# Block 2's tokens loaded as bands and turned by DMA transposes, as in the later blocks

## The chip, the cores and the metric

The kernel runs on one core of a Trainium2 chip. The metric is the device time of that core in microseconds. A core has TensorE (PE) for matmuls, VectorE (DVE), ScalarE (ACT), GpSimd (POOL) and SyncE (SP), and 16 DMA engines that move data between HBM and the on-chip memory. GpSimd, SyncE and ScalarE issue the transfers. Each engine works through its own instructions in order and waits on semaphores for the others.

## What is computed

Chunked attention, and a gated feed-forward layer on its output. There are 4 batches, 8 heads, 768 tokens and head size 64:

```python
for c in range(nc):                       # chunks of 32 queries
    l_start = max(0, 32 * c - 16)
    r_end = min(S, 32 * c + 32 + 8)
    k_full = concatenate([mem_k, k[:, :, l_start:r_end]])     # 8 memory rows + up to 56 keys
    v_full = concatenate([mem_v, v[:, :, l_start:r_end]])
    a = softmax(q_c @ k_full.T / sqrt(D))
    out[:, :, chunk] = a @ v_full
x = out as (3072 tokens, 512)
result = (maximum(x @ w_gate, 0) * (x @ w_val)) @ w_out       # w_gate, w_val 512x1536, w_out 1536x512
```

Inputs and output are float32. The kernel computes with float16 operands and float32 sums.

## The kernel before

The 3072 tokens are cut into 8 blocks of 384 (`TB`), two to a batch. A block's queries are four pieces of 96 (`NQ`, `QB`), and each piece looks at one window of 8 memory rows and 120 tokens, which fills the 128 partitions. Heads are handled as four pairs (`hp`).

*Feed-forward.* A block takes twelve units (`ffn_unit`), one for each 128 columns of the hidden layer: four gate matmuls and four value matmuls (L380), a Relu on ScalarE (L388, `gr`), and a product on VectorE (L392, `gv`). Three out units (`out_unit`, L416) then multiply `gv` with `wo`, copy the result on ScalarE and store it. The weights `wg`, `wv` and `wo` stay on chip. `wo` is loaded in three pieces of 512 KB.

*Attention.* For a head pair the steps are: scores and exponentials (`step_s`), values and sums with the logarithm of the sums (`step_v`: L344, L348), the reciprocal (`step_e`, L353), and the product into `xT` (`step_m`, L359). `xT` is what the block's units read. The attention of block n+1 is spread over the units of block n by `run(order, n, at, turn_at)`: `at[hp]` names the unit after which a pair's scores are computed. Values come two units later and the product three units later.

*How K and Q get their transposed form* differs between blocks.

- Blocks 0, 1 and 2 load rows of four tokens (`load_rows`: `rk`, `rq`). TensorE turns them with matmuls against selection matrices (`turn_k`, `turn_q`, L207), and VectorE copies the result (`copy_k`, `copy_q`, tile `kq`). Their scores are eight matmuls for a pair (`score_mms`, L263), each over the 64 rows of one head.
- Blocks 3 to 7 load windows of tokens (`load_band` and `load_q_tokens`: tiles `k16`, shown as `k`, and `q16n`; L145, L171). SyncE turns them by DMA transposes (`turn_dma`: `kT`, `qT`; L241, L243). GpSimd copies `qT` into a block-diagonal tile `qbd` (`spread_q`, L250), whose other halves were cleared once (`clear_q`, L659). The scores are then four matmuls for a pair over all 128 rows (L287).

*What sets the order.* The order is written by hand: under `manual_schedule` every engine runs its instructions in program order. Blocks 0 and 1 follow a list of named steps (`go`), and after them come the calls of `run`. All float32-to-float16 loads are issued by GpSimd, so its program order is also the order of these loads. A load waits for the landing of the load eight before it. `spread_q` stands in this same order. Block 2 is the only later block that is turned by matmuls inside `run`: its turns sit between the gate and value matmuls of block 1's units 1, 4, 7 and 10 (`turning`), and its scores follow units 2, 5, 8 and 11. GpSimd's order around the change is: block 2's rows, block 2's V (`vwin`), the three pieces of `wo`, block 3's K, q and V, and block 3's `spread_q`.

Of the kernel before, what the change touches and what calls it, by code (L numbers as in the profile page):

```python
# [8 lines left out]
F32 = mybir.dt.float32  # L9
# [8 lines left out]
def kernel(  # L18
# [99 lines left out]
    def rows_of(n):  # L118
        if n not in rows:
            rows[n] = (half.tile([KR + 2, H, J * D], F16, tag="rk", name="rk"),  # L120
                       half.tile([QR, H, J * D], F16, tag="q16", name="rq"))
        return rows[n]

    def load_rows_mem(dma, dst, n, h0, nh, src_t=mem_k):
        src = bass.AP(tensor=src_t.tensor, offset=src_t[n // 2, h0, 0, 0].offset,
                      ap=[[J * D, 2], [NMEM * D, nh], [1, J * D]])
        dma(dst, src)
# [7 lines left out]
    def load_rows(n, h0, nh):  # L135
        load_k(n, h0, nh)
        load_q(n, h0, nh)

    def load_band(n, src_t, dsts):
        b, p = divmod(n, 2)  # L140
        for i in range(NQ):
            m0, m1 = (16 if (p == 0 and i == 0) else 0), (112 if (p == 1 and i == NQ - 1) else BAND)
            src = bass.AP(tensor=src_t.tensor, offset=src_t[b, 0, TB * p + QB * i - 16 + m0, 0].offset,
                          ap=[[D, m1 - m0], [S * D, H], [1, D]])
            pool_dma(dsts[p][NMEM + m0:NMEM + m1, i, :, 0:D], src)  # L145
# [12 lines left out]
    def load_mem_v(n):  # L158
        b, p = divmod(n, 2)
        for i in range(NQ):  # L160
            sp(vwins[p][0:NMEM, i, :, 0:D], memv[:, H * b:H * b + H, :])
# [11 lines left out]
    def load_w(c0, c1):  # L173
        for dst, src in ((wg, moe_w_gate), (wv, moe_w_val)):
            pool_dma(dst[:, :, c0:c1], src.rearrange("(c p) f -> p c f", p=128)[:, :, c0:c1])
# [8 lines left out]
        return pools["f"].tile([128, 512], F32, tag="f", name=name)  # L184

    def turn_k(n, hp):
        if n != 1:
            pool, tag = (pools["t"], "t") if n == 0 else (pools["s"], "sc")
            ps = pool.tile([128, 2, 512], F32, tag=tag, name="kq_ps")
            kps, qps = ps[:, 0], xs if (n, hp) == (0, 0) else ps[:, 1, 0:TB]  # L190
        else:
            ps, kps, qps = None, bank("k_ps"), bank("q_ps")[:, 0:TB]
        turns[n, hp] = ps, kps, qps


        steps = kps.rearrange("p (i j t) -> p j i t", i=NQ, j=J) if n < 2 else kps.rearrange("p (j r) -> p j r", j=J)
        turn_mms(rows_of(n)[0], steps, sels[n % 2].rearrange("p i t -> p (i t)")[0:KR + 2], hp)

    def turn_q(n, hp):
        steps = turns[n, hp][2].rearrange("p (r j) -> p j r" if n == 0 else "p (j r) -> p j r", j=J)  # L200
# [2 lines left out]
    def turn_mms(t, steps, w, hp):  # L203
        t = t.rearrange("p h (j d) -> p h j d", j=J)
        for j in range(J):
            for hh in range(2):
                nc.tensor.matmul(steps[D * hh:D * hh + D, j], lhsT=t[:, 2 * hp + hh, j], rhs=w,  # L207
                                 start=True, stop=True)

    def kq_of(n):  # L210
        if n not in kTs:
            kq = turned.tile([128, HP, 512 + TB], F16, tag="kq", name="kq")
            kTs[n] = kq[:, :, 0:512].rearrange("p a (i m) -> p i a m", i=NQ)
            qTs[n] = kq[:, :, 512:].rearrange("p a (i m) -> p i a m", i=NQ)
            turns[n] = kq
        return turns[n]

    def copy_k(n, hp):
        src, dst = turns[n, hp][1], kq_of(n)[:, hp, 0:512]
        if n == 2:  # L220
            src, dst = src.rearrange("p (j r) -> p r j", j=J), dst.rearrange("p (r j) -> p r j", j=J)
        dve_copy(dst, src)  # L222

    def copy_q(n, hp):
        src, dst = turns[n, hp][2], kq_of(n)[:, hp, 512:]
# [4 lines left out]

    def copy_kq(hp):
        dve_copy(kq_of(0)[:, hp], turns[0, hp][0].rearrange("p a c -> p (a c)")[:, 0:512 + TB])

    def turn(n, hp):
        for step in (turn_k, turn_q, copy_k, copy_q):
            step(n, hp)

    def turn_dma(n):
        kTs[n] = turned.tile([128, NQ, HP, 128], F16, tag="kT", name="kT")
# [39 lines left out]

    def score(n, hp):  # L280
        sc = scs[n, hp] = pools["s"].tile([128, 2, 512], F32, tag="sc", name="sc_ps")
        if n < 3:
            score_mms(n, hp, sc, True)
        else:

            for i in range(NQ):
                nc.tensor.matmul(sc[:, i // 2, 192 * (i % 2):192 * (i % 2) + 192], lhsT=kTs[n][:, i, hp, :],  # L287
                                 rhs=qbds[n % 2][:, i, hp].rearrange("p h m -> p (h m)"), start=True, stop=True)

    def score_exp(n, hp):  # L290
        view = scs[n, hp][:, :, 0:TB].rearrange("p a (c m) -> p a c m", m=QB)
        if n < 3:
            flat = exs[n, hp] = epool.tile([128, 2, NQ, QB], F16, tag="ex", name="ex")
        else:
            ex = epool.tile([128, NQ, 2, QB], F16, tag="ex", name="ex")
            flat, exs[n, hp] = ex.rearrange("p (a b) h m -> p a (b h) m", b=2), ex.rearrange("p i h m -> p h i m")
        for g in range(3):
            s = slice(32 * g, 32 * g + 32)
            nc.scalar.activation(flat[:, :, :, s], view[:, :, :, s], ACT.Exp, scale=SCALE,  # L299
                                 bias=(bias1 if n == 1 else bias)[:, g:g + 1])  # L300
# [127 lines left out]
    def unit(n, u, between=()):  # L428
        if u < NDC:
            ffn_unit(n, u, between)  # L430
        else:
            out_unit(n, u - NDC, between)
# [14 lines left out]
    def words(t):  # L447
        return t.bitcast(U32)
# [42 lines left out]
    def load_v_rows(n):  # L491
        r0 = 0 if n == 0 else S // J - KR
        for h0 in (0, 4):
            pool_dma(rv[0:KR, h0:h0 + 4], bass.AP(tensor=v.tensor, offset=v[0, h0, J * r0, 0].offset,
                                                  ap=[[J * D, KR], [S * D, 4], [1, J * D]]))
# [9 lines left out]

    ONE = 0x3C003C00


    def chunk(n, f):
        for x in range(2):  # L510
# [87 lines left out]
    def go(steps):  # L598
        for step in steps.split():
            name = step.rstrip("0123456789")  # L600
            STEPS[name](int(step[len(name):]))
# [12 lines left out]
    with tc.tile_pool(name="tps", bufs=3, space=bass.MemoryType.PSUM) as pools["t"]:  # L614
# [13 lines left out]
    load_w(512, 768)  # L628
    load_w(768, 1024)
    load_v_rows(1)  # L630
    load_w(1024, 1280)
    load_w(1280, 1536)
    fetch_mem(memv, mem_v)
    fetch_mem(memk, mem_k)
    load_rows_mem(pool_dma, rows_of(2)[0][KR:KR + 2], 2, 0, H)
    load_rows(2, 0, 4)
    load_rows(2, 4, 4)

    go("""
        Vb1 mb0 Vb3 Vb2 mb1 ch0 Eb3 ch1 mb2 mb3 ch2 ch3 r0 r1 g2 v2 mu0 r2 T0 mu1 g3 cq0 v3 ck0 T2 r3 mu2 mu3  # L640
# [1 line left out]

    zero(vwins[0][0:NMEM + 16, 0, :, 0:D], 0.0)
    load_mem_v(2)
    go("""
        cq2 ck2 T1 ck1 S0 g4 e0 cq1 v4 r4 S1 D0 mu4 T3 e1 L0 g6 S2 e2 v6 ck3 D1 cq3 r6 E0 g5 mu6 L1 r5 S3 v5 g7
        v7 mu5 e3 r7 g9 mu7 E1 D2 G0 r9 g8 v9 L2 cg0 mu9 v8 G1 D3 cg1 E2 r8 g11 V0 v11 L3 r11 mu8 m0 V1 g10 m1
        V2 m2 V3 E3 m3 v10 mu11 r10 mu10
    """)
    zero(vwins[1][96:128, NQ - 1, :, 0:D], 0.0)  # L650
    load_band(2, v, vwins)
    wo_src = moe_w_out.rearrange("(c p) f -> p c f", p=128)
    for a in range(0, NDC, 4):
        pool_dma(wo[:, a:a + 4, :], wo_src[:, a:a + 4, :])


    def clear_q(p, hh):
        w = words(qbds[p].rearrange("p i a h m -> p (i a h m)")).rearrange("p (i a h m) -> p i a h m", i=NQ, a=HP, h=2)
        zero(w[D * hh:D * hh + D, :, :, 1 - hh, :].rearrange("p i a m -> p (i a) m"), 0)  # L659

    def window0_ones():
        one_words(0, 0, 128, 0, 1, ONE)
# [3 lines left out]
    clear = [window0_ones, lambda: one_words(0, 0, 128, 1, 2, ONE), lambda: one_words(0, 0, 128, 2, NQ, ONE),  # L666
             lambda: one_words(1, 0, 128, 0, NQ, ONE),
             lambda: (one_words(1, 96, 128, NQ - 1, NQ, 0), one_words(1, 96, 120, NQ - 1, NQ, ONE))]
    clear += [lambda p=p, hh=hh: clear_q(p, hh) for p in range(2) for hh in range(2)]


    STEP = {"s": step_s, "v": step_v, "e": step_e, "m": step_m}
# [1 line left out]
    def pieces(n, what):  # L674
        for w, hp in what:
            STEP[w](n, hp)
# [3 lines left out]
    def run(order, n, at, turn_at):  # L680
        for u, (b, x) in enumerate(order):
            now = [hp for hp in range(HP) if n < NB and u == at[hp] + 2]
            if n < NB:
                pieces(n, [("m", hp) for hp in range(HP) if u == at[hp] + 3])
            inner, outer = ("ve", "") if x >= NDC else ("v", "e")
            turning = [hp for hp in range(HP) if n == 2 and u == at[hp] - 1]
            unit(b, x, [lambda hp=hp: turn(n, hp) for hp in turning]
                 + [lambda w=(w, hp): pieces(n, [w]) for hp in now for w in inner])
            pieces(n, [(w, hp) for hp in now for w in outer])
            if n < NB:  # L690
                pieces(n, [("s", hp) for hp in range(HP) if u == at[hp]])
            if n == 2 and u < len(clear):
                clear[u]()
            if u == turn_at and n + 1 < NB:
                turn_dma(n + 1)
                spread_q(n + 1)

    def loads(n):
        if n < NB:
            load_mem_k(n)  # L700
            load_band(n, k, k16s)
            load_q_tokens(n)
            load_band(n, v, vwins)
            load_mem_v(n)

    loads(3)
    run([(1, m) for m in range(NDC)] + [(b, NDC + t) for b in range(2) for t in range(NT)], 2, (2, 5, 8, 11), 13)
    for n in range(2, NB):
        loads(n + 2)
        run([(n, u) for u in range(NDC + NT)], n + 1, (0, 3, 6, 9), 9)  # L710
# [30 lines left out]
```

The softmax here doesn't subtract the row's maximum and nothing guards it: scores larger than these inputs give would overflow.

## Time and profile before

The time is 236.66 us, the median of 3 runs (236.61 to 236.88). The profiled execution spans 235.7 us with a granted TensorE clock of 1.00 throughout.

| stretch (us from the start) | what runs | PE busy (us) | GB/s moved |
|---|---|---|---|
| 0.0 to 25.5 | loads, block 0's attention | 21.36 | 183 |
| 25.5 to 40.7 | block 0's units, block 1's attention | 15.20 | 180 |
| 40.7 to 62.2 | block 1's units, block 2's turns and attention | 20.74 | 169 |
| 62.2 to 78.1 | six out units of blocks 0 and 1 | 15.90 | 155 |
| 78.1 to 104.3 | block 2's units and outs, block 3's attention | 26.20 | 126 |
| 182.5 to 208.5 | block 6's units and outs, block 7's attention | 26.00 | 31 |

In the lines below, an instruction has its start, its duration, the engine, the line, the operation, and the tiles as out<-in. What it waited for stands in brackets: the idle time before it and the instruction that ended it. A line "x4" is four instructions in a row.

### The profile page before, as it was taken

The page shows a single profiled execution, that of the slowest core. Times are in us where ns is not written, and L with a number is a line of the kernel's source. Part 1 is how long each engine was busy: PE and PEld are TensorE (multiplying, and loading weights), DVE is VectorE, ACT ScalarE, POOL GpSimd, SP SyncE. Part 2 cuts the span into 40 slices and gives each one's busy share as a digit, 9 for nine tenths or more (in the row PEclk, how much of TensorE's full clock was granted, in tenths as well). Part 3 has the DMA queues.
Part 4 walks back from the last instruction along what each step waited for, and adds up shares of the span by engine and source line. Part 5 has one row for each costly group of instructions (what it writes and reads, how often), then busy time and mean ns, then how long its engine had stood idle before and what let it go on. Part 6 is the DMA issues. An engine that isn't in the chain of part 4 may idle for free.

```text
span 235.7 us, 4736 instructions
## 1 busy us (share of the span) xinstructions
PE 227.0 (96%) x1807; PEld 131.2 (56%) x1807; DVE 109.9 (47%) x214; ACT 141.0 (60%) x300; POOL 96.6 (41%) x124
## 2 busy tenths in 40 slices
PE   7799899998999999999999999999999999999993
PEld 3455455555544666556664666556654666456641
DVE  4685647889810156504652166305461266214400
ACT  3483793477652489628882699547882798433310
POOL 8786557927079403980089306950130000000000
PEclk9999999999999999999999999999999999999999
DMA  7999999999939992999919991999902100120012
GB/s 166 171 195 196 196 188 157 176 185 149 175 112 166 192 177 56 74 170 137 154 11 156 173 172 26 107 168 177 77 0 92 45 0 3 45 89 3 1 46 89
DMA packets 101033, 27.53 MB, mean 117 GB/s; under 512 B 83122, under 2 KB 98066, under 8 KB 101010
## 3 DMA queue, kind: packets, MB, share of 16 engines
q0 software_dynamic: 76336, 15.12, 77.6%
q1 hardware_dynamic: 20802, 5.55, 18.8%
q10 hardware_dynamic: 3872, 6.56, 8.4%
q8 instruction: 14, 0.23, 0.4%
q14 instruction: 9, 0.07, 0.1%
HBM read 31.06 MB, written 6.29 MB: 159 GB/s over the span
## 4 chain that ended last, share of the span: by engine, by line
PE 84%; DMA 11%; DVE 2%; issue 1%; ACT 0%; POOL 0%; POOLq 0%
PE o_ps L416 25%; PE g_ps L380 25%; PE v_ps L380 25%; DMA wv<-in_moe_w_val_dram 4%; DMA wg<-in_moe_w_gate_dram 3%; DMA rk<-in_k_dram 3%; PE sc_ps L287 3%; PE xo_ps L344 2%; PE xs_ps L344 2%; DMA out_dram<-o_sb 1%; PE sc_ps L263 1%; PE kq_ps L207 1%; DVE gv L392 1%; DVE qbd L659 1%; DVE kq L222 1%
## 5 line engine op out<-in xcount | busy, mean ns | idle before, releaser
L392 DVE TENSOR_TENSOR gv<-v_ps,gr 128x384 f16<-128x384 f32 x95 | 52.6, 555 | 94.2 <-ACT gr L388 82.9
L380 PE MATMUL v_ps<-xT,wv 128*128 128x384 f16 x380 | 78.2, 326 | 0.5 <-DMA wv<-in_moe_w_val_dram 0.5
L380 PE MATMUL g_ps<-xT,wg 128*128 128x384 f16 x380 | 78.4, 326 | 0.1
L416 PE MATMUL o_ps<-wo,gv 128*128 128x512 f16 x288 | 63.5, 379 | 0.0
L388 ACT ACTIVATE gr<-g_ps 128x384 f16<-128x384 f32 x95 | 46.1, 487 | 19.1 <-PE g_ps L380 10.3
L380 PEld LDWEIGHTS <-wg 128*128 128x128 f16 x384 | 36.5, 98 | 22.8 <-DMA wg<-in_moe_w_gate_dram 0.3
L380 PEld LDWEIGHTS <-wv 128*128 128x128 f16 x384 | 35.8, 98 | 22.3 <-DMA wv<-in_moe_w_val_dram 0.9
L416 PEld LDWEIGHTS <-gv 128*128 128x128 f16 x288 | 28.1, 98 | 32.9
L250 POOL COPY qbd<-qT 64x1536 f16<-64x1536 f16 x10 | 14.6, 1462 | 59.3 <-DMA qT<-q16n 59.0
L425 ACT COPY o_sb<-o_ps 128x512 f32<-128x512 f32 x23 | 13.5, 585 | 39.2 <-PE o_ps L416 33.2
L299 ACT ACTIVATE ex<-sc_ps,bias 128x256 f16<-128x256 f32 x84 | 33.3, 468 | 4.6 <-PE sc_ps L263 3.8
L145 POOL DMA_DIRECT2D vwin<-in_v_dram x24 | 21.7, 929 | 2.0 <-DVE gv L392 1.3
L353 ACT ACTIVATE rinv<-ln,mln 64x768 f32<-64x768 f32 x24 | 22.1, 923 | 0.0
L348 ACT ACTIVATE ln<-xo_ps 64x384 f32<-64x384 f32 x24 | 11.7, 487 | 16.5 <-PE xs_ps L344 16.5
L145 POOL DMA_DIRECT2D k<-in_k_dram x20 | 17.9, 909 | 0.0
L359 DVE TENSOR_TENSOR xT<-xo_ps,rinv 64x384 f16<-64x384 f32 x24 | 13.1, 547 | 9.8 <-ACT rinv L353 9.7
L171 POOL DMA_DIRECT2D q16n<-in_q_dram x20 | 15.6, 798 | 4.9 <-DMA wo<-in_moe_w_out_dram 4.9
L359 DVE TENSOR_TENSOR xT<-xs_ps,rinv 64x384 f16<-64x384 f32 x24 | 13.2, 551 | 0.7
L344 PEld LDWEIGHTS <-vwin 128*128 128x128 f16 x192 | 10.6, 98 | 3.0
L348 ACT ACTIVATE ln<-xs_ps 64x384 f32<-64x384 f32 x24 | 11.4, 475 | 0.0
L344 PE MATMUL xo_ps<-ex,vwin 128*128 128x96 f16 x96 | 11.1, 206 | 0.0
L344 PE MATMUL xs_ps<-ex,vwin 128*128 128x96 f16 x96 | 11.1, 206 | 0.0
(89 smaller groups left out, 140.3 us busy)
## 6 DMA issues: line engine op xcount, KB each, us to landing
out_dram<-o_sb ACTq DMA_DIRECT2D x23, 256.0 KB
vwin<-in_v_dram POOLq DMA_DIRECT2D x18, 120.0 KB, 10.0
q16n<-in_q_dram POOLq DMA_DIRECT2D x20, 96.0 KB, 5.1
k<-in_k_dram POOLq DMA_DIRECT2D x15, 120.0 KB, 4.2
wg<-in_moe_w_gate_dram POOLq DMA_DIRECT2D x6, 256.0 KB, 9.0
wv<-in_moe_w_val_dram POOLq DMA_DIRECT2D x6, 256.0 KB, 9.3
wo<-in_moe_w_out_dram POOLq DMA_DIRECT2D x3, 512.0 KB, 8.6
rk<-in_k_dram POOLq DMA_DIRECT2D x5, 224.0 KB, 6.8
```

The lines of the kernel that those rows point to most:

```text
L145: pool_dma(dsts[p][NMEM + m0:NMEM + m1, i, :, 0:D], src)
L171: pool_dma(q16s[n][:, i], src)
L250: nc.gpsimd.tensor_copy(qbds[n % 2][s, :, :, hh, :].rearrange("p i a m -> p (i a) m"), qTs[n][s].rearrange("p i a m -> p (i a) m"))
L299: nc.scalar.activation(flat[:, :, :, s], view[:, :, :, s], ACT.Exp, scale=SCALE, bias=(bias1 if n == 1 else bias)[:, g:g + 1])
L344: nc.tensor.matmul((xo, xs)[hh][:, QB * i:QB * i + QB], lhsT=vw[:, i, 2 * hp + hh, :], rhs=ex[:, hh, i, :], start=True, stop=True)
L348: nc.scalar.activation(ln[:, hh], (xo, xs)[hh][D:128], ACT.Ln, scale=1.0 / 64.0)
L353: nc.scalar.activation(rinv, lns.pop((n, hp)), ACT.Exp, scale=-1.0, bias=mln64[0:D, :])
L359: nc.vector.tensor_tensor(out=x_of(n)[D * hh:D * hh + D, hp, :], in0=(xo, xs)[hh][0:D], in1=rinv[:, hh, :], op=ALU.mult)
L380: nc.tensor.matmul(ps[a], lhsT=(wg, wv)[a][:, f, 128 * m:128 * m + 128], rhs=xTs[n][:, f, :], start=(f == 0), stop=(f == NFC - 1))
L388: nc.scalar.activation(grs[n, m], g_ps, ACT.Relu)
L392: nc.vector.tensor_tensor(out=gvs[n][:, m, :], in0=v_ps, in1=grs.pop((n, m)), op=ALU.mult)
L416: nc.tensor.matmul(o_ps, lhsT=gvs[n][:, m, 128 * t:128 * t + 128], rhs=wo[:, m, :], start=(m == 0), stop=(m == NDC - 1))
```

## The change

Block 2 is prepared like blocks 3 to 7. GpSimd issues its K as four band loads and its q as four token loads, where the rows stood, and V after that. SyncE does its DMA transposes (`turn_dma(2)`) after the copies of its memory rows. `spread_q(2)` fills `qbd`, and is placed after block 3's K and q loads. The two halves of the first `qbd` are cleared by GpSimd instead of VectorE, between loads of V rows and weights. Block 2's scores become four matmuls for a pair. The turns, their copies and their helper functions go. As its K and q are meant to come through longer steps, block 2's attention moves from units 2, 5, 8 and 11 of block 1 to units 9, 11, 13 and 14, of which 12 and later are out units. The purpose is to take the turning matmuls off TensorE and their copies off VectorE.

```diff
     def score(n, hp):
-        if n < 3:
+        if n < 2:
             score_mms(n, hp, sc, True)
...
     def score_exp(n, hp):
-        if n < 3:
+        if n < 2:
...
     load_v_rows(1)
+    for hh in range(2):
+        clear_q(0, hh, nc.gpsimd.memset)
     load_w(1024, 1280)
     load_w(1280, 1536)
     fetch_mem(memv, mem_v)
     fetch_mem(memk, mem_k)
-    load_rows_mem(pool_dma, rows_of(2)[0][KR:KR + 2], 2, 0, H)
-    load_rows(2, 0, 4)
-    load_rows(2, 4, 4)
+    load_mem_k(2)
+    load_band(2, k, k16s)
+    load_q_tokens(2)
...
     load_mem_v(2)
+    turn_dma(2)
+    load_band(2, v, vwins)
...
     zero(vwins[1][96:128, NQ - 1, :, 0:D], 0.0)
-    load_band(2, v, vwins)
...
-    clear += [lambda p=p, hh=hh: clear_q(p, hh) for p in range(2) for hh in range(2)]
+    clear += [lambda hh=hh: clear_q(1, hh, zero) for hh in range(2)]
...
-            turning = [hp for hp in range(HP) if n == 2 and u == at[hp] - 1]
-            unit(b, x, [lambda hp=hp: turn(n, hp) for hp in turning]
-                 + [lambda w=(w, hp): pieces(n, [w]) for hp in now for w in inner])
+            unit(b, x, [lambda w=(w, hp): pieces(n, [w]) for hp in now for w in inner])
...
-    loads(3)
-    run([(1, m) for m in range(NDC)] + [(b, NDC + t) for b in range(2) for t in range(NT)], 2, (2, 5, 8, 11), 13)
+    load_mem_k(3)
+    load_band(3, k, k16s)
+    load_q_tokens(3)
+    spread_q(2)
+    load_band(3, v, vwins)
+    load_mem_v(3)
+    run([(1, m) for m in range(NDC)] + [(b, NDC + t) for b in range(2) for t in range(NT)], 2, (9, 11, 13, 14), 15)
```

More of the change, by code (lines that the diff above doesn't have):

```diff
@@ L186, in turn_k @@
     def turn_k(n, hp):
-        if n != 1:
-            pool, tag = (pools["t"], "t") if n == 0 else (pools["s"], "sc")
-            ps = pool.tile([128, 2, 512], F32, tag=tag, name="kq_ps")
+        if n == 0:
+            ps = pools["t"].tile([128, 2, 512], F32, tag="t", name="kq_ps")
             kps, qps = ps[:, 0], xs if (n, hp) == (0, 0) else ps[:, 1, 0:TB]
@@ L193, in turn_k @@
         turns[n, hp] = ps, kps, qps
-        steps = kps.rearrange("p (i j t) -> p j i t", i=NQ, j=J) if n < 2 else kps.rearrange("p (j r) -> p j r", j=J)
-        turn_mms(rows_of(n)[0], steps, sels[n % 2].rearrange("p i t -> p (i t)")[0:KR + 2], hp)
+        steps = kps.rearrange("p (i j t) -> p j i t", i=NQ, j=J)
+        turn_mms(rows_of(n)[0], steps, sels[n].rearrange("p i t -> p (i t)")[0:KR + 2], hp)
     def turn_q(n, hp):
@@ L218, in copy_k @@
     def copy_k(n, hp):
[L219 to L222, printed above, removed]
+        dve_copy(kq_of(n)[:, hp, 0:512], turns[n, hp][1])
     def copy_q(n, hp):
@@ L232, in copy_kq @@
         dve_copy(kq_of(0)[:, hp], turns[0, hp][0].rearrange("p a c -> p (a c)")[:, 0:512 + TB])
-    def turn(n, hp):
-        for step in (turn_k, turn_q, copy_k, copy_q):
-            step(n, hp)
     def turn_dma(n):
@@ L506, with clear_q @@
     ONE = 0x3C003C00
+    def clear_q(p, hh, zero_):
+        w = words(qbds[p].rearrange("p i a h m -> p (i a h m)")).rearrange("p (i a h m) -> p i a h m", i=NQ, a=HP, h=2)
+        zero_(w[D * hh:D * hh + D, :, :, 1 - hh, :].rearrange("p i a m -> p (i a) m"), 0)
     def chunk(n, f):
@@ L654 @@
         pool_dma(wo[:, a:a + 4, :], wo_src[:, a:a + 4, :])
-    def clear_q(p, hh):
-        w = words(qbds[p].rearrange("p i a h m -> p (i a h m)")).rearrange("p (i a h m) -> p i a h m", i=NQ, a=HP, h=2)
-        zero(w[D * hh:D * hh + D, :, :, 1 - hh, :].rearrange("p i a m -> p (i a) m"), 0)
     def window0_ones():
```

## The prediction

> **What bounds the kernel now.** I read the page's busy shares first, then the chain of waits, then TensorE's and GpSimd's timelines from 40 to 80 us, where the change lies. Busy shares:
>
> ```profile
> PE 227.0 (96%) x1807; PEld 131.2 (56%) x1807; DVE 109.9 (47%) x214; ACT 141.0 (60%) x300; POOL 96.6 (41%) x124
> ```
>
> TensorE is the bound and leaves 8.7 us of idle time in the whole span. The chain of waits says the same after 25.5 us, when the first weights are in: only matmuls, apart from a short stretch (start, duration, what):
>
> ```profile
> 16.39 9.06 DMA wv<-in_moe_w_val_dram
> 25.49 0.82 PE v_ps L380 x4
> ...
> 55.34 0.69 DVE kq L222
> 57.06 0.70 DVE qbd L659
> ...
> 62.32 3.99 PE o_ps L416 x18
> 66.65 11.65 PE o_ps L416 x54
> ```
>
> So the change can gain what it takes out of TensorE's row between 40.72 us (block 1's first unit) and 78.14 us (block 2's first), 37.42 us. What one turn of block 2 costs there, on TensorE's timeline:
>
> ```profile
> 42.02 0.81 PE L380 MATMUL g_ps<-xT,wg 128*128 128x384 f16 x4
> 42.77 0.41 PE L207 MATMUL kq_ps<-sel,rk 114*64 114x128 f16 x8
> 43.01 0.34 PE L207 MATMUL kq_ps<-ident,rq 96*64 96x96 f16 x8
> 43.28 0.82 PE L380 MATMUL v_ps<-xT,wv 128*128 128x384 f16 x4
> ...
> 56.56 0.34 PE L263 MATMUL sc_ps<-kq 64*128 64x96 f16 x8 [0.66 <-DVE kq L229]
> ```
>
> The gate starts at 42.02, the value matmuls at 43.28: 1.26 us, of which the gate is 0.65; the turn is 0.61. The last line is a wait on VectorE's copy.
>
> The other half is GpSimd's timeline, which is also the order of all loads:
>
> ```profile
> 40.41 2.28 POOL L654 DMA_DIRECT2D wo<-in_moe_w_out_dram  x3
> 42.65 3.62 POOL L145 DMA_DIRECT2D k<-in_k_dram  x4
> 46.22 0.84 POOL L171 DMA_DIRECT2D q16n<-in_q_dram  x1
> 47.57 0.77 POOL L171 DMA_DIRECT2D q16n<-in_q_dram  x1 [0.51 <-DMA wo<-in_moe_w_out_dram]
> 50.07 0.77 POOL L171 DMA_DIRECT2D q16n<-in_q_dram  x1 [1.73 <-DMA wo<-in_moe_w_out_dram]
> 53.46 0.77 POOL L171 DMA_DIRECT2D q16n<-in_q_dram  x1 [2.62 <-DMA wo<-in_moe_w_out_dram]
> ...
> 66.21 2.98 POOL L250 COPY qbd<-qT 64x1536 f16<-64x1536 f16 x2 [7.70 <-DMA qT<-q16n]
> ```
>
> A load cannot be issued until the one eight before it has landed: the second, third and fourth q load of block 3 each wait for one of the three wo pieces. The last wo piece landed at 53.46 us. Today nothing hurries: after that wait come the V loads and a copy needed only at 79.44.
>
> [...] kT and qT take 4.3 and about 5 us in the quiet stretch 56.54 to 66.2, and 14.8 us in 77.07 to 91.85, beside the V loads. [...] here they moved 278 to 282 GB/s alone (windows 61:62, 64:65.5), so I use that. [...] at the launch: the first five fill matmuls took 1.78 us, the next nine 2.12[...].
>
> Prices from the windows view, GB/s moved: 195 for rows and weights (21:31), 200 for wo (44:50), 153 for band loads (53:58), 148 to 159 when transposes, band loads and output stores mix (77:92, 101.5:118.5, 128.8:143.4, 153:170).
>
> **Part 1, turns and scores on TensorE.** Removed: 4 turns x 0.61 = 2.44 us. Four 8-matmul scores become 4-matmul ones: g starts 78.14, v 78.79, score 79.44, next g 79.77, so 0.33 each, against 0.37 (44.60 to 45.62 less 0.65): 0.16 us. The waits on kq (0.66, and about 0.3 before the last score) go. Checked from below: 12 units x 1.30 + 6 out units x 2.59 (7.77 for three) + 4 x (0.33 + 0.35 for the V matmuls) = 33.85, so 37.42 - 33.85 = 3.6 us gained if nothing waits. VectorE loses 8 copies and two clears, off the chain once the turns are gone.
>
> **Part 2, clears on GpSimd.** Two memsets of 64x768 words stand before the last weight loads. VectorE's took 0.70 us; scaling GpSimd's 128x64-word memsets, which start 0.08 us apart, by 12 gives 0.96; its 64x1536 f16 copy took 1.46. So 1.4 to 2.9 us for both; I take 2. That delays an issue at 21.30, but the next one already waits 1.21 us for a landing and weights land 9 us after issue: the DMA backlog hides it.
>
> **Part 3, the loads.** Block 2's 832 KB (0.85 MB) of rows become bands of the same size: 0.85 MB / 195 GB/s = 4.4 us become 0.87 / 153 = 5.7, +1.3 us. All sits ahead of wo in the load queue, and the page's DMA row shows its top digit from 6 to about 60 us.
>
> **Part 4, DMA transposes of block 2.** The last weight load (wv, issued at 25.73) landed near 36.5: the load eight behind it, the first vwin, left GpSimd at 36.46. Block 2's K is next in the queue, 0.48 MB at 153 GB/s, 3.1 us, so it lands near 40; SyncE is through with the memory V copies, which stand ahead of the transposes, at 36.60 + 3.13 = 39.7. So kT and qT (0.92 MB) start about 40 to 43 us, beside the V band and wo, which are queued then. They push wo back by between 0.92/280 = 3.3 us and 0.92/153 = 6.0 us. I take 6.0, since every stretch in which they mixed with band loads stayed near 153 GB/s. Last wo piece: 53.46 + 1.3 + 6.0 = 60.8 us.
>
> **Part 5, a new wait.** In the changed GpSimd order stand: K, q and V of block 2, wo, K and q of block 3, then block 2's two qbd copies. The copies do not depend on wo, but they stand behind block 3's last q load, which must wait for the last wo piece. So: 60.8 + 0.77 (issue) + 2.98 (two copies) = 64.5 us. The scores of head pair 0 contract all 128 partitions, so need both copies; they stand after unit 9, at 40.72 + 10 x 1.30 = 53.7 us. On TensorE units 10, 11 and all six out units are queued behind them: a stall of 64.6 - 53.7 = 10.9 us. ScalarE and VectorE wait with it; block 3's V loads are behind the copies as well.
>
> **Part 6, the clock.** [...] 1.5 us lost[...].
>
> **Part 7, after it.** Units 10, 11 and outs take 20.8 us from the score: block 2 starts at 64.6 + 20.8 + 1.5 = 86.9. Block 3's qbd: q landing about 66, transposes 10 to 14.5 us beside V loads, copy 3: 79 to 83.5, wanted at 86.9 + 1.3. In time. Later blocks keep their cycle (copies started at 91.85, 118.53, 143.37: about 26 us, like TensorE's 26.05), so nothing is given back or added.
>
> Sum: 236.66 - 3.6 + 10.9 + 1.5 = 245.5 us.
>
> **Rivals.** (a) Mild contention: transposes pass at their own 280 GB/s, wo lands at 53.46 + 1.3 + 3.3 = 58.1, stall 8.2, clock 1.5: 242.8; without a clock loss 241.3. For: the quiet stretch. Against: wo is queued just then. (b) Severe: wo only starts when transposes that take 14.8 us from 40.2 are done, 55, and needs 1.57 MB / 200 = 7.9, so 63 to 65, stall 13 to 15: 247.6 to 249.6. For: the mixed stretches later. (c) Faster: qbd is ready before 53.7 and only Part 1 is left: 236.66 - 3.6 = 233.1. For: block 2's q lands about 42. Against: GpSimd's order and the waits at 47.57, 50.07 and 53.46. (d) No change: wo as early as now, 53.46 + 3.75 = 57.2, stall 3.5 against 3.6 gained: 236.6. Against: more bytes ahead of it in a full queue. This is the floor of the stall as long as the load waits for wo.
>
> **How the numbers follow.** Forecast 0.55, (a) 0.22, (b) 0.16, (c) 0.04, (d) 0.03. Part 3 alone is uncertain by 1 us, the clock by 1.5. Low 240.5: (a) without clock loss less about 1 us; high 250: (b). Faster 0.04, same 0.02 (most of (d); its rest is slower), slower 0.94.
>
> **What would show it.** Right: TensorE's one long gap before the first qbd score, at 53.7, 8 to 15 us, with GpSimd's qbd copies just before its end and q16n's waits on wo before them; wo landing at 58 to 65; DMA near 150 GB/s while kT and qT run; no L207 kq_ps matmuls after 30 us[...]. Wrong: q16n waits ending by 53, or copies before 54, which means (c); block 3's score waiting too, which makes Part 7 wrong and the time longer; weights g8 to g11 waiting after 33 us, which makes Part 2 wrong.

## The result and the profile after

The changed kernel takes 246.08 us (median of 4 runs) beside 236.63 for the kernel before: 9.45 us more. The ratio is 1.0386, with a 95% interval of 1.0357 to 1.0415. Medians here and below are over all runs, ratios over those in the chip's faster state; one of these four runs, at 251.27 us, was in a slower one, and by the ratio the change costs 9.1 us. The forecast was 245.5 us.

From the page of the changed kernel, TensorE's busy time and two rows of 40 slices (about 6.1 us each, in tenths): TensorE's busy share and its granted clock.

```profile
PE 227.3 (93%) x1727; PEld 131.5 (54%) x1727; DVE 105.0 (43%) x204; ACT 142.4 (58%) x300; POOL 104.0 (43%) x131
...
PE   7999999970699999999999999999999999999994
...
PEclk9999999996599999999999999999999999999999
```

Eighty matmuls are gone (1807 to 1727), yet the busy time has not fallen and the share has, from 96% to 93%. There is one hole, from the end of the ninth slice into the eleventh, and the clock is low in the tenth and eleventh. TensorE's timeline shows the hole:

```profile
52.71 0.81 PE L372 MATMUL v_ps<-xT,wv 128*128 128x384 f16 x4
63.44 0.80 PE L279 MATMUL sc_ps<-qbd,kT 128*128 128x192 f16 x4 [9.91 <-POOL qbd L242]
64.03 1.49 PE L372 MATMUL g_ps<-xT,wg 128*128 128x384 f16 x4
65.31 1.49 PE L372 MATMUL v_ps<-xT,wv 128*128 128x384 f16 x4
```

L279 is the block-diagonal score and L372 a unit's matmul, L287 and L380 of the kernel before. The first score of block 2 waits 9.91 us for GpSimd's `qbd`. After it four matmuls of 384 columns take 1.28 us from start to start (64.03 to 65.31) where they took 0.65. GpSimd's timeline says what came before:

```profile
42.11 2.28 POOL L653 DMA_DIRECT2D wo<-in_moe_w_out_dram  x3
...
52.99 0.77 POOL L171 DMA_DIRECT2D q16n<-in_q_dram  x1 [1.67 <-DMA wo<-in_moe_w_out_dram]
56.37 0.77 POOL L171 DMA_DIRECT2D q16n<-in_q_dram  x1 [2.61 <-DMA wo<-in_moe_w_out_dram]
59.59 0.77 POOL L171 DMA_DIRECT2D q16n<-in_q_dram  x1 [2.45 <-DMA wo<-in_moe_w_out_dram]
60.41 2.98 POOL L242 COPY qbd<-qT 64x1536 f16<-64x1536 f16 x2
...
74.54 2.99 POOL L242 COPY qbd<-qT 64x1536 f16<-64x1536 f16 x2 [7.63 <-DMA qT<-q16n]
```

`wo` leaves GpSimd 1.7 us later than before and its last piece lands at 59.59 us, 6.1 us later (53.46). Block 2's copies follow the last q load at once. They end at 63.39, and the score starts at 63.44. SyncE's timeline has block 2's two transposes from 40.41 on:

```profile
40.41 4.25 SPq L233 DMA_TRANSPOSE kT<-k  x1
44.85 5.13 SPq L235 DMA_TRANSPOSE qT<-q16n  x1
```

The windows view gives two-microsecond stretches (stretch, length, busy time of TensorE, of its weight loads, VectorE, ScalarE and GpSimd, granted clock, DMA share, GB/s):

```profile
56.00:58.00 2.00, 0.00 (x0) 0.00 (x0) 0.00 (x0) 0.00 (x0) 0.77 (x1) 0.77 1.21 195
58.00:60.00 2.00, 0.00 (x0) 0.00 (x0) 0.00 (x0) 0.00 (x0) 0.41 (x1) 0.50 1.67 170
...
64.00:66.00 2.00, 2.00 (x9) 0.98 (x8) 0.00 (x0) 1.65 (x4) 2.00 (x3) 0.50 1.86 119
66.00:68.00 2.00, 2.00 (x16) 1.20 (x15) 0.56 (x1) 0.05 (x1) 0.90 (x2) 0.67 1.51 202
```

The DMA engines work all through the hole (148 to 196 GB/s in the two-microsecond windows from 54 to 64 us), and the clock goes to 0.50. Windows of 0.2 us place the fall between 57.0 and 57.2 us, 3.5 us into the pause, and the return between 67.2 and 67.4, 3.9 us after its end.

From block 1's first unit to block 2's first the row is 87.04 - 40.36 = 46.7 us, against 37.4. The parts the prediction had for it are 33.85 of matmuls and the pause, 9.9. There are 1.9 of slow matmuls (next section), and about 0.8 in the last out units, where a pair's values wait for the products of the pair before.

### The profile page after: what moved, and what is told of

Its sections match the earlier page's. It is cut to its first block, busy times and chain, and to the rows that moved or that the text cites. A ratio compares the mean times of both kernels' runs of the same rounds, so it can differ in the third digit from the quotient of the medians.

```text
span 244.4 us, 4586 instructions
## 1 busy us (share of the span) xinstructions
PE 227.3 (93%) x1727; PEld 131.5 (54%) x1727; DVE 105.0 (43%) x204; ACT 142.4 (58%) x300; POOL 104.0 (43%) x131
## 4 chain that ended last, share of the span: by engine, by line
PE 73%; DMA 15%; POOL 6%; issue 2%; ACT 2%; DVE 1%; ACTq 0%; POOLq 0%
PE o_ps L408 23%; PE g_ps L372 22%; PE v_ps L372 21%; DMA k<-in_k_dram 7%; DMA wv<-in_moe_w_val_dram 4%; DMA wg<-in_moe_w_gate_dram 3%; PE sc_ps L279 3%; PE xs_ps L336 2%; PE xo_ps L336 2%; POOL wo L653 1%; POOL vwin L145 1%; DMA out_dram<-o_sb 1%; POOL q16n L171 1%; POOL qbd L242 1%; POOL rv L486 1%
## 5 line engine op out<-in xcount | busy, mean ns | idle before, releaser
L372 PE MATMUL g_ps<-xT,wg 128*128 128x384 f16 x380 | 79.4, 330 | 0.0
L372 PE MATMUL v_ps<-xT,wv 128*128 128x384 f16 x380 | 78.8, 328 | 0.5 <-DMA wv<-in_moe_w_val_dram 0.5
L380 ACT ACTIVATE gr<-g_ps 128x384 f16<-128x384 f32 x95 | 46.3, 488 | 24.0 <-PE g_ps L372 12.9
L372 PEld LDWEIGHTS <-wg 128*128 128x128 f16 x384 | 37.1, 99 | 23.3 <-issue 1.2
L372 PEld LDWEIGHTS <-wv 128*128 128x128 f16 x384 | 36.2, 98 | 23.0 <-DMA wv<-in_moe_w_val_dram 0.9
L242 POOL COPY qbd<-qT 64x1536 f16<-64x1536 f16 x12 | 17.6, 1464 | 58.1 <-DMA qT<-q16n 57.7
L291 ACT ACTIVATE ex<-sc_ps,bias 128x256 f16<-128x256 f32 x84 | 33.4, 469 | 15.3 <-PE sc_ps L279 10.9
L145 POOL DMA_DIRECT2D k<-in_k_dram x24 | 21.5, 904 | 3.0 <-DMA vwin<-in_v_dram 1.4
L171 POOL DMA_DIRECT2D q16n<-in_q_dram x24 | 18.6, 778 | 9.2 <-DMA wo<-in_moe_w_out_dram 6.7
L279 PE MATMUL sc_ps<-qbd,kT 128*128 128x192 f16 x96 | 12.1, 250 | 9.9 <-POOL qbd L242 9.9
L279 PEld LDWEIGHTS <-kT 128*128 128x128 f16 x96 | 8.8, 99 | 13.5 <-issue 10.3
```

The costliest lines, as they stand in the source:

```text
L171: pool_dma(q16s[n][:, i], src)
L242: nc.gpsimd.tensor_copy(qbds[n % 2][s, :, :, hh, :].rearrange("p i a m -> p (i a) m"), qTs[n][s].rearrange("p i a m -> p (i a) m"))
L372: nc.tensor.matmul(ps[a], lhsT=(wg, wv)[a][:, f, 128 * m:128 * m + 128], rhs=xTs[n][:, f, :], start=(f == 0), stop=(f == NFC - 1))
L380: nc.scalar.activation(grs[n, m], g_ps, ACT.Relu)
```

## The experiments

Two theories could explain the hole. In the first, GpSimd's order is the cause: the copies have their data, but stand behind a load that waits for `wo` (the prediction's part 5). In the second, the DMA engines are the cause: `qT` lands no earlier than `wo`, since both share them. Each time below stands beside the median of the kernel before, measured with it on the same chip.

**The copies put first.**

```diff
+    spread_q(2)
     load_mem_k(3)
     load_band(3, k, k16s)
     load_q_tokens(3)
-    spread_q(2)
     load_band(3, v, vwins)
```

> Only block 2's two qbd copies move: they now stand ahead of block 3's K and q loads on GpSimd, so they no longer wait for the load that waits for wo. Theory A (the place in GpSimd's order causes the gap, as step 5 of the prediction has it): qT is there well before wo, the copies end at 55 to 58 us, the gap before the first qbd score shrinks from 9.9 to 3 to 5 us, time 239 to 242 us. Theory B (the DMA engines cause it: qT shares them with wo packet by packet and lands when wo does, near 59.5 us): the copies end near 62.4, the gap shrinks by about 1 us, time 244.5 to 246 us.

247.18 us beside 236.84, ratio 1.0404 (1.0362 to 1.0446), not to be told from the changed kernel's 1.0386. GpSimd's timeline:

```profile
42.77 2.31 POOL L653 DMA_DIRECT2D wo<-in_moe_w_out_dram  x3
60.47 2.98 POOL L242 COPY qbd<-qT 64x1536 f16<-64x1536 f16 x2 [15.38 <-DMA qT<-q16n]
...
86.86 2.98 POOL L242 COPY qbd<-qT 64x1536 f16<-64x1536 f16 x2 [13.23 <-DMA qT<-q16n]
```

Nothing stands ahead of the copies now, and they still start at 60.47: GpSimd waits 15.38 us for `qT`. So the wait for `qT` is enough for the hole, as the second theory says, and GpSimd's order is not its only cause. The sizes that this theory expected were missed: TensorE's gap is 10.7 us, longer than the changed kernel's 9.9 and not 1 us shorter, and the time is over 246. Block 3 now gets its loads later and waits too, 1.76 us for the second pair of copies.

Why `qT` lands so late can be read in the DMA view of the changed kernel's trace from 56 to 58 us, queue by queue (packets, MB, share of the 16 engines' time). Queue q0 carries `wo` there and q1 the transposes:

```profile
q0 software_dynamic: 305, 0.31, 91.5%
q1 hardware_dynamic: 305, 0.08, 29.5%
```

Both queues move the same number of packets, but those of `wo` have 1 KB and those of the transposes about 256 bytes. So `wo` moves 155 GB/s and the transposes 40, where they moved 278 to 282 alone in the kernel before (61 to 62 and 64 to 65.5 us).

**The pause filled.**

```diff
+            if n == 2 and u == at[0]:
+                fill(58)
             if n < NB:
                 pieces(n, [("s", hp) for hp in range(HP) if u == at[hp]])
```

> 58 fill matmuls on zeros (128x384, 0.163 us each, 9.5 us) are put on TensorE ahead of the first qbd score, inside the gap. Clock theory (step 6): the score and the following unit run at full rate, 0.65 instead of 1.28 us for four matmuls, 1.9 us less: 244.0 to 244.5 us. Rival (the slow matmuls after the gap are a ramp that the fill does not prevent, or the fill lengthens the gap): 246 us or more.

244.63 us beside 236.84, ratio 1.0311 (1.028 to 1.0341). TensorE's timeline:

```profile
53.66 9.59 PE L429 MATMUL xo_ps<-filler 128*128 128x384 f16 x58
63.44 0.49 PE L279 MATMUL sc_ps<-qbd,kT 128*128 128x192 f16 x4 [0.19 <-POOL qbd L242]
...
85.16 0.81 PE L372 MATMUL g_ps<-xT,wg 128*128 128x384 f16 x4
```

The score starts at 63.44 as in the changed kernel, but block 2 starts at 85.16 instead of 87.04. So the low clock costs 1.88 us, and work without use in the pause takes that back: the granted clock is 1.00 in every window from 36 to 68 us. The time is 0.1 us above the range expected. GpSimd's timeline of this run also shows the two waits of the copies one after the other:

```profile
59.46 0.77 POOL L171 DMA_DIRECT2D q16n<-in_q_dram  x1 [2.49 <-DMA wo<-in_moe_w_out_dram]
60.41 2.98 POOL L242 COPY qbd<-qT 64x1536 f16<-64x1536 f16 x2 [0.18 <-DMA qT<-q16n]
```

The load that waited for `wo` is issued by 60.23, and `qT` lands 0.18 us after that.

**The transposes left out.**

```diff
-    turn_dma(2)
     load_band(2, v, vwins)
...
+    kTs[2] = turned.tile([128, NQ, HP, 128], F16, tag="kT", name="kT")
+    qTs[2] = turned.tile([128, NQ, HP, QB], F16, tag="qT", name="qT")
+    for t in (kTs[2], qTs[2]):
+        zero(words(t.rearrange("p i a m -> p (i a m)")), 0)
     load_mem_k(3)
```

> Leaves out block 2's two DMA transposes: kT and qT of block 2 are set to zero by VectorE (two memsets, about 1.6 us), all loads stay. So block 2's attention output is wrong and only the time is read. Transpose theory (steps 3 and 4: bands cost wo 1.3 us, transposes 6): last wo piece lands at 52.5 to 55 us instead of 59.6, the copies end 3.8 us later, 56 to 59, time 237 to 241 us. Rival (the small band packets delay wo, not the transposes): wo lands at 57 us or later, time 243 us or more.

242.56 us beside 236.84, ratio 1.023 (1.0192 to 1.0268). This lies between the two expectations, nearer to the rival. GpSimd's timeline:

```profile
39.45 3.63 POOL L145 DMA_DIRECT2D vwin<-in_v_dram  x4
43.04 2.31 POOL L652 DMA_DIRECT2D wo<-in_moe_w_out_dram  x3
...
56.92 0.77 POOL L171 DMA_DIRECT2D q16n<-in_q_dram  x1 [1.75 <-DMA wo<-in_moe_w_out_dram]
57.73 2.98 POOL L242 COPY qbd<-qT 64x1536 f16<-64x1536 f16 x2
```

And its windows:

```profile
36.00:40.00 4.00, 4.00 (x55) 2.19 (x52) 3.18 (x5) 1.97 (x4) 3.64 (x5) 1.00 1.90 126
40.00:44.00 4.00, 4.00 (x27) 2.38 (x26) 3.52 (x8) 1.24 (x3) 4.00 (x6) 1.00 1.93 129
```

Without transposes `wo` lands at 56.92: 2.7 us sooner than in the changed kernel, but still 3.5 us later than before. The copies now start as soon as the load that waits for `wo` is issued, and TensorE's gap is 6.77 us: GpSimd's order, too, is enough for a hole by itself. The shares are less sure than 3.5 and 2.7 look. `wo` was issued at 43.04 here and at 42.11 in the changed kernel. From the first issue to the last landing it takes 13.05 us in the kernel before, 13.88 here and 17.48 in the changed kernel. Counted so, the loads cost 2.5 us and the transposes 3.6.

GpSimd is busy for 3.64 and 4.00 us of these two stretches, almost all of it issuing loads of 0.8 to 0.9 us each, and the engines move 126 to 129 GB/s, not the 153 assumed. Block 2's eight K and q loads at 0.8 to 0.9 us have taken the place of five row loads at 0.56 to 0.73. The trace fits a limit at the issue. I did not isolate it from the packet size.

**The clears alone, on the kernel before.** Rows, turns and scores are those of the kernel before, and only the four clears move.

```diff
     def clear_q(p, hh):
...
-        zero(w[D * hh:D * hh + D, :, :, 1 - hh, :].rearrange("p i a m -> p (i a) m"), 0)
+        nc.gpsimd.memset(w[D * hh:D * hh + D, :, :, 1 - hh, :].rearrange("p i a m -> p (i a) m"), 0)
...
     load_v_rows(1)
+    for hh in range(2):
+        clear_q(0, hh)
...
     load_rows(2, 4, 4)
+    for hh in range(2):
+        clear_q(1, hh)
...
-    clear += [lambda p=p, hh=hh: clear_q(p, hh) for p in range(2) for hh in range(2)]
```

> The kernel before with one part of the change alone: the four qbd clears (0.70 us each on VectorE, between the turns' copies) move to GpSimd. If the two waits of TensorE on kq copies (0.66 and about 0.3 us) come from the clears in VectorE's row, time falls by 0.5 to 0.9 us, to 235.7 to 236.2. If the copies are late anyway, or GpSimd's 3 us delay its loads, no change (236.6) or slower.

235.73 us beside 236.84, ratio 0.9956 (0.9939 to 0.9973): 1.1 us less than the kernel before, as expected, and faster than both kernels. TensorE's timeline, at the place where the score used to wait 0.66 us:

```profile
53.90 0.81 PE L380 MATMUL v_ps<-xT,wv 128*128 128x384 f16 x4
54.65 0.34 PE L263 MATMUL sc_ps<-kq 64*128 64x96 f16 x8
```

The score follows the unit at once. From block 1's first unit to block 2's (39.54 to 76.06) the row takes 36.5 us instead of 37.4, which is the size of the two waits. That gain needs no change of block 2's loads. The change itself moves two of the four clears, and there are no copies of `kq` left there for them to delay.

**The order changed, V held back.** SyncE's transposes go first, `wo` follows block 2's q loads, the copies follow `wo`, and scores come after units 11 to 14.

```diff
-    load_mem_v(2)
     turn_dma(2)
-    load_band(2, v, vwins)
+    load_mem_v(2)
...
-    load_mem_k(3)
-    load_band(3, k, k16s)
-    load_q_tokens(3)
     spread_q(2)
+    load_band(2, v, vwins)
+    load_mem_k(3)
+    load_band(3, k, k16s)
+    load_q_tokens(3)
     load_band(3, v, vwins)
...
-    run([(1, m) for m in range(NDC)] + [(b, NDC + t) for b in range(2) for t in range(NT)], 2, (9, 11, 13, 14), 15)
+    run([(1, m) for m in range(NDC)] + [(b, NDC + t) for b in range(2) for t in range(NT)], 2, (11, 12, 13, 14), 15)
```

> The changed kernel with four places moved: SyncE issues block 2's transposes ahead of its memory rows of V (3 us sooner); GpSimd's order is block 2's K and q, wo, block 2's qbd copies, then block 2's V and block 3's loads, so nothing but wo shares the engines with the transposes; scores after units 11, 12, 13, 14. DMA-capacity theory: wo at 153 and transposes at 155 packets a microsecond end near 50 and 53 us, copies end at 55 to 57, scores are wanted at 56.4, so a gap below 2 us and no clock loss: 233.5 to 236 us, unless block 3's qbd comes late (its loads leave GpSimd 6 us later), which adds 1 to 3 us. Rival (transposes are slow by themselves, whatever runs beside them): qT lands after 57 us, gap of 4 us or more, 239 us or more.

247.94 us beside 236.91, ratio 1.0442 (1.04 to 1.0483). No gain; the 233.5 to 236 us expected are a miss. TensorE's timeline:

```profile
59.78 0.49 PE L279 MATMUL sc_ps<-qbd,kT 128*128 128x192 f16 x4 [3.75 <-POOL qbd L242]
...
88.33 0.80 PE L279 MATMUL sc_ps<-qbd,kT 128*128 128x192 f16 x4 [4.48 <-POOL qbd L242]
```

The first wait falls from 9.9 to 3.75 us, but the loads that were held back make block 3's score wait 4.48. The out units wait in more places, and both pauses cost clock: its mean is 0.57 from 60 to 64 us, and after the second pause four matmuls of 384 columns take 1.28 us from start to start (88.92 to 90.20). The wait has moved. It has not gone. The rival, that transposes are slow whatever runs beside them, does not hold: their queue, which moves 40 GB/s beside `wo` in the changed kernel, moved 278 to 282 alone in the kernel before, and with V loads beside them the copies start 4.2 us later than here (next experiment).

**The same with V ahead of the copies.** The edit is against the kernel of the last experiment.

```diff
+    load_band(2, v, vwins)
     spread_q(2)
-    load_band(2, v, vwins)
     load_mem_k(3)
```

> As the reordered kernel with wo ahead of V, but block 2's V loads leave GpSimd before the qbd copies instead of after them, so they share the DMA engines with the transposes. DMA-capacity theory: qT lands 2 to 4 us later than with V held back, gap 2 to 5 us, time 1 to 4 us above that kernel. Rival (V's place does not matter to the transposes): the same time, or better since V is there earlier.

247.48 us beside 236.91, ratio 1.043 (1.04 to 1.0459). The time is the same, so the expected 1 to 4 us are a miss. The mechanism is seen: the copies start at 60.98 us here, when `qT` lands, and at 56.75 with V held back, where the engines move 179 GB/s from 52 to 56 us and only 19 from 56 to 60. So sharing with the V loads costs about 4.2 us. It is paid in the first gap (8.06 us) instead of at block 3.

**Only the scores later.**

```diff
-    run([(1, m) for m in range(NDC)] + [(b, NDC + t) for b in range(2) for t in range(NT)], 2, (9, 11, 13, 14), 15)
+    run([(1, m) for m in range(NDC)] + [(b, NDC + t) for b in range(2) for t in range(NT)], 2, (11, 12, 13, 14), 15)
```

> The changed kernel with only its scores moved from units 9, 11, 13, 14 to 11, 12, 13, 14: loads and transposes as they are. If qbd comes when DMA brings it (60.4 us plus 3 for the copies) and nothing before the scores sets that, 2 units (2.6 us) run ahead of the gap, which falls from 9.9 to about 7.3 us: 243 to 244 us. Rival (later scores also make the out units wait for values, products and the logarithms): 245 us or more.

245.56 us beside 236.91, ratio 1.0347 (1.0312 to 1.0382). By the ratios that is 8.2 us above the kernel before, where the changed kernel is 9.1 above: the direction expected, but not the size, and the intervals overlap. 243 to 244 us were expected, and the time is nearer to the rival's. What takes it stays open.

**Block 2's K and q left out.** This gives the ceiling of the idea: TensorE's order as in the changed kernel, with nothing to wait for.

```diff
-    for hh in range(2):
-        clear_q(0, hh, nc.gpsimd.memset)
+    nc.gpsimd.memset(words(qbds[0].rearrange("p i a h m -> p (i a h m)")), 0)
...
-    load_mem_k(2)
-    load_band(2, k, k16s)
-    load_q_tokens(2)
...
-    turn_dma(2)
...
+    kTs[2] = turned.tile([128, NQ, HP, 128], F16, tag="kT", name="kT")
+    zero(words(kTs[2].rearrange("p i a m -> p (i a m)")), 0)
...
-    spread_q(2)
```

> Leaves out block 2's K and q loads, its DMA transposes and its qbd copies: kT is set to zero by VectorE and the whole first qbd by GpSimd, so block 2's scores are zeros and only the time is read. TensorE's order is that of the changed kernel. Step 1 of the prediction (3.6 us of TensorE's row gained, once nothing waits): 233 to 234 us, with a wait of 0.5 to 1 us in the out units for products of the pair before. Rival (the late attention in the out units costs as much as the turns): 235.5 us or more.

234.52 us beside 236.93, ratio 0.9901 (0.9872 to 0.993). This lies between the two expectations. TensorE's timeline, with block 1's first unit, a wait in the last out units, and block 2's first unit:

```profile
40.11 0.81 PE L372 MATMUL g_ps<-xT,wg 128*128 128x384 f16 x4
...
70.63 0.22 PE L336 MATMUL xs_ps<-ex,vwin 128*128 128x96 f16 x1 [0.38 <-DVE xT L351]
...
74.82 0.81 PE L372 MATMUL g_ps<-xT,wg 128*128 128x384 f16 x4
```

The row takes 74.82 - 40.11 = 34.7 us instead of 37.4: 2.7 us gained. The forecast of 3.6 lacked the wait for products, which comes with the attention in the out units: from 69.8, where the out matmuls before it end, to 70.94, where the next begin, there are 1.15 us with 0.35 us of value matmuls in them. That is 0.8 us lost. Of the 2.7 gained, about 0.9 are the waits that the clears alone remove.

**The first clears back on VectorE.**

```diff
-    for hh in range(2):
-        clear_q(0, hh, nc.gpsimd.memset)
...
-    clear += [lambda hh=hh: clear_q(1, hh, zero) for hh in range(2)]
+    clear = [lambda p=p, hh=hh: clear_q(p, hh, zero) for p in range(2) for hh in range(2)][0:2] + clear + [lambda hh=hh: clear_q(1, hh, zero) for hh in range(2)]
```

> The changed kernel with one part undone: the first qbd's two clears return from GpSimd (1.54 us at 20.7 us) to VectorE, after block 1's first units. Step 2 (the clears on GpSimd hide behind the DMA backlog): the same time as the changed kernel, 245.5 to 247, qT and wo landing as there. Rival (1.5 us of GpSimd ahead of the weights push every later load): qbd 1 to 1.5 us sooner, 244.5 to 245.

247.5 us beside 236.93, ratio 1.0429 (1.0379 to 1.048). It is no faster than the changed kernel (the intervals overlap, and the time is 0.5 us above the range expected), and the last `wo` lands at 60.25 us, no sooner. No cost of the GpSimd clears is seen, as part 2 said.

## Why the prediction was right

The total was right, and so was the path: TensorE stands before the first `qbd` score until GpSimd's late copies are done. One of the two waits that make them late was missing, and some terms were off in opposite directions.

| part | predicted | measured |
|---|---|---|
| 1, row gained | 3.6 us | 2.7, with K and q left out |
| 2, clears on GpSimd | about 2 us, hidden | 1.54, hidden |
| 3, K and q loads push `wo` | 1.3 us | 2.5 to 3.5, with no transposes |
| 4, transposes push `wo` | 6.0 us | 2.7 to 3.6, the rest of 6.1 |
| 5, last `wo`, copies end, gap | 60.8, 64.5, 10.9 us | 59.59, 63.39, 9.91 |
| 6, low clock | 1.5 us | 1.88, with the pause filled |
| 7, block 3 in time | ready 79 to 83.5 us | ready 77.5, wanted at 88.34 |
| sum | +8.8 us | +9.45 (9.1 by the ratio) |

With the measured terms the sum is -2.7 + 9.9 + 1.9 = 9.1 us. That the forecast came within 0.6 us of the median is in part luck: the gap was 1.0 us too long and the gain 0.9 too large, and the two nearly cancel.

- *Part 1* held up to the 0.8 us wait for products in the out units, which it had at zero.
- *Parts 3 and 4* came to 7.3 us together where 6.1 were measured, and their shares were wrong by either count: the loads cost more than 1.3 us, the transposes less than 6.0. The price of 153 GB/s for the loads was read from a stretch with a full queue. Where GpSimd has to issue eight of them in a row, the rate is 126 to 129. The price for the transposes took every byte as if it queued ahead of `wo`. They ran beside it instead, at 195 GB/s for both; what they cost `wo` is near the 3.3 us of rival (a). The sign "DMA near 150 GB/s while kT and qT run" did not come: the windows from 42 to 58 us have 90 to 196.
- *Part 5* saw one of two waits: "The copies do not depend on wo, but they stand behind block 3's last q load, which must wait for the last wo piece." The trace shows this wait, and without the transposes it alone holds the copies until 57.73 us. But the prediction had `qT` in time and gave it no wait. With the copies put first they start no sooner, since `qT`, issued at 44.85 in the changed kernel, lands only near 60.4 us. The time was right because the two waits end within 0.2 us of each other. That is luck: nothing in part 5 reckoned when `qT` lands. The floor of rival (d) holds only as long as the load waits for `wo`, and says nothing of this second wait.
- *Part 6* held in kind: work at a granted clock of 0.50 was seen behind the pause, and its cost was measured by itself, 1.88 us. The 1.5 us were the author's estimate; nothing in the trace of the kernel before shows what such a pause costs. The windows give 3.5 us until the clock falls and 3.9 until it is back. With the copies put first, mean clocks of 0.53 from 56 to 60 us and 0.69 from 64 to 68 put the fall 3.4 to 3.5 us into the pause and the return 3.0 us after its end.
- *Rivals.* Mild contention (242.8) and severe (247.6 to 249.6) were both passed by. "Faster" needed `qbd` by 53.7 us and was 9.7 us away from it. The kernel with K and q left out shows how little it could have brought, 2.4 us.

## What to carry to other kernels

Work taken off the bounding engine is worth only what its replacement can deliver in time. Here 2.7 us of TensorE's row were traded for 0.9 MB of DMA transposes and eight loads that take longer to issue, in a stretch where 1.57 MB of `wo` had to pass as well. Before giving another buffer's cause to a queue position, ask when the waiting instruction's own input lands: moving the instruction is a cheap test, and two waits that end together, 0.2 us apart here, look like one in a profile. And a change made of parts may hold one good part: the clears, moved alone in the kernel before, beat both kernels.

## What the runs showed of the hardware

The transposes and `wo` share the engines at nearly the total rate of `wo` alone: 195 GB/s from 56 to 58 us, and 200 from 44 to 50 in the kernel before, where 1.16 of 1.20 MB were on the queue of `wo`. But in each two microseconds from 50 to 58 the two queues moved the same number of packets to within one, 305 to 319 each, and not the same bytes: 0.08 MB in the small packets of the transposes and 0.31 in the larger ones of `wo`, or 40 and 155 GB/s. The transposes then take far longer: with the copies first, block 2's pair was issued from 40.92 and through at 60.47, 19.6 us, where block 3's pair in the kernel before took 56.54 to 66.21, 9.7 us. V loads were issued around the start of both pairs (39.17 to 42.80 and 54.59 to 58.51), and in the kernel before their queue still moved 0.16 MB from 58 to 60 us and 0.23 from 62 to 64, so that the prediction's "quiet stretch" was not wholly quiet; `wo` ran beside the first pair only. In the reordered kernel the issue of `kT` alone held SyncE for 9.34 us, against 4.25 to 5.93 in the timelines up to 90 us of the kernel before and the changed one.

The clock fell after a pause of 3.75 us, too. In the reordered kernel that pause ended at 59.78, and the mean clock is 1.00 from 56 to 60 us and 0.57 from 60 to 64. How long it stayed low once work went on differed: 3.9 us in the changed kernel, 3.0 with the copies put first.
